# Loading the first batch, w1 and w2 ahead of w3 and w_out, and forming W3·w_out after the first chunk's stage one

## The chip, the cores and the metric

The kernel runs on one core of one Trainium2 chip. The metric is the device time of one execution in microseconds (us). Five engines work side by side, each through its own list of instructions in order: TensorE (PE, with its weight loads as PEld), VectorE (DVE), ScalarE (ACT), GpSimd (POOL) and SyncE (SP), which here issues nearly all DMAs.

## The reference

Attention with a softmax on q along the head dimension and a softmax on k along the sequence, and then a multiplicative feed-forward network on the result:

```python
q_s = softmax(q, axis=-1); k_s = softmax(k, axis=2)      # per batch and head
kv  = einsum('bhsd,bhse->bhde', k_s, v)
x   = einsum('bhsd,bhde->bhse', q_s, kv)                 # 8 batches, 8 heads, 576 x 64
x   = x.transpose(0, 2, 1, 3).reshape(4608, 512)
out = (((x @ w1) * (x @ w2)) @ w3) @ w_out               # d_ff = 1024, float32 out
```

## The kernel before

Everything is computed in f16 with f32 sums in PSUM. The product W3·w_out (1024 x 512, called W3O here, in eight tiles) is formed once, so that the network is two stages: stage one (`s1`) makes a·b for 512 tokens from x and 128 columns of w1 and of w2; stage two (`s2`) multiplies it by W3O for 128 tokens and stores them. The 4608 tokens are nine chunks of 512; they straddle the eight batches of 576.

**Attention of one batch.** Heads lie in two halves i = 0, 1 of four. `exp_q`, `exp_k` (ScalarE, L121 and L114), `sum_q` (VectorE, L133), `norm_q` (a reciprocal at L138 and a product on GpSimd at L140, tile eqn), `cast_v` (v to f16, L126). The normalised q is transposed into qsT, for batch 0 on TensorE (`piece_t`, L175, with a copy at L177) and for all others by a DMA transpose that SP issues (`dma_t`, L180). `piece_kv` (L154) makes kv, which VectorE normalises (L159, L163); `piece_x` (L192) makes x transposed, and ScalarE or VectorE copies it to the tile xT (L198, L200). `pieces(b)` are kv, x of half 0 and x of half 1.

**The weights.** w1 and w2 come in quarters of 256 columns (`load_w12`, L87), and are cast in four blocks each by three engines (`cast_w`, L94). w3 comes in eight row tiles (`load_w3`, L105), is cast (`w3_c`, L280), transposed on TensorE (`w3_t`, L292, copy at L297) and multiplied by the cast w_out (`wo_c`, L286) in `w3_mm` (L302).

**What sets the order.** The order is written by hand (`manual_schedule`): each engine does its instructions in the order of the program text. All loads pass through one ring of 12 staging slots ("st"); a load waits until the slot of the twelfth load before it has been read. Each DMA of SP also waits for the eighth DMA before it. In PSUM there are two "att" buffers of two banks each (transposes, kv, x), three "pab" buffers (stage one, W3O, alternate s2 tiles) and one "po". `warm(n)` are matmuls on zeros (L210) that nothing reads.

Before, SP issues w3 and w_out first (L311 to L318), then batch 0 (L355), w1 and w2 (L374), batch 1 (L398), the transposes of batch 1 (L444), batch 2 (L446). TensorE forms W3O while these arrive (L327 to L365), then does the attention of batch 0 (L379 to L401), stage one of chunk 0 with the exponentials of batch 1 between its last tiles (L421 to L443), and s2 of chunk 0 with kv and x of batch 1 between (L448 to L463).

From chunk 1 on, a loop (L506) runs eight s1 tiles and, one chunk behind, four s2 tiles; after each of these 12 places it calls `step()` (L471). A step takes the next of ten elementwise pieces of a batch (six for q, four for k and v), and puts the later work of the batch into `due`: its `dma_t` three steps after the product, loads, and `pieces` some steps after the tenth. Two steps are made ahead of the loop (L501).

Of the kernel before, what the change touches and what calls it, by code (L numbers as in the profile page):

```python
# [8 lines left out]
F32 = mybir.dt.float32  # L9
# [7 lines left out]
def kernel(  # L17
# [11 lines left out]
    nc = tc.nc  # L29
# [3 lines left out]
    P = 128  # L33
# [3 lines left out]
    N_FT = Fd // P  # L37
# [21 lines left out]
    def pAtt(shape, dtype):  # L59
        return psum.tile(shape, dtype, tag="att", name="att", bufs=2)  # L60

    def pAB():
        return psum.tile([P, CH], F32, tag="pab", name="pab", bufs=3)

    def pO():
        return psum.tile([P, C], F32, tag="po", name="po", bufs=1)
# [7 lines left out]
    def load_qkv(b, which, i, halves=False):  # L74
        src = {"q": q, "k": k, "v": v}[which]
        t = slot([P, 2, R * D])
        ap = src[b, 4 * i:4 * i + 4].rearrange("(h g) (s r) d -> (g s) h (r d)", g=2, r=R)
        for sl in (slice(0, 1), slice(1, 2)) if halves else (slice(0, 2),):
            nc.sync.dma_start(out=t[:, sl], in_=ap[:, sl])
        qkv32[(which, b, i)] = t  # L80
# [22 lines left out]
    def load_w3(ft):  # L103
        t = slot([P, Fd])
        nc.sync.dma_start(out=t, in_=moe_w3[ft * P:(ft + 1) * P, :])  # L105
        w32[("3", ft)] = t
# [11 lines left out]
    def exp_q(b, i, hh):  # L118
        if hh == 0:
            eqs[(b, i)] = attn.tile([P, R, 2, D], F16, tag="eq", name="eq", bufs=2)  # L120
        nc.scalar.activation(  # L121
            out=eqs[(b, i)][:, :, hh, :],
            in_=qkv32[("q", b, i)][:, hh].rearrange("p (r d) -> p r d", r=R), func=AF.Exp)
# [80 lines left out]
                lambda: (piece_x(b, 0, 0, 5), piece_x(b, 0, 5, 9)),  # L204
                lambda: (piece_x(b, 1, 0, 5), piece_x(b, 1, 5, 9, *[vcopy][b > 2:]))]

    def warm(n, att=False):
        wp = pAtt([P, 2, CH], F32)[:, 0] if att else pAB()
        for _ in range(n):
            nc.tensor.matmul(wp, lhsT=zero[:, 0:P], rhs=zero, start=True, stop=True)  # L210

# [63 lines left out]
    def w3_c(ft, *copies):  # L275
        w316s[ft] = attn.tile([P, Fd], F16, tag="w316", name="w316", bufs=3)
        n = Fd // len(copies)
        for m, copy in enumerate(copies):
            sl = slice(m * n, (m + 1) * n)
            copy(out=w316s[ft][:, sl], in_=w32[("3", ft)][:, sl])  # L280

    def wo_c(i, *copies):
        n = C // len(copies)
        for m, copy in enumerate(copies):
            sl = slice(m * n, (m + 1) * n)
            copy(out=wosb[i][:, :, sl], in_=w32[("o", i)][:, :, sl])  # L286

    def w3_t(ft):
        w316 = w316s[ft]
        tp = pAtt([P, N_FT, P], F16)  # L290
        for gt in range(N_FT):
            nc.tensor.transpose(tp[:, gt, :], w316[:, gt * P:(gt + 1) * P], ident)  # L292
        if ft < 4:
            w3T = attn.tile([P, R, P], F16, tag="qsT", name="qsT", bufs=4)
        else:
            w3T = attn.tile([P, R, P], F16, tag="eqn", name="eqn", bufs=4)
        nc.vector.tensor_copy(out=w3T[:, 0:N_FT, :], in_=tp)  # L297
        w3Ts[ft] = w3T

    def w3_mm(wps, ft, gts):  # L300
        for gt in gts:
            nc.tensor.matmul(wps, lhsT=w3Ts[ft][:, gt, :], rhs=wosb[gt // 2][:, gt % 2, :],  # L302
                             start=(gt == 0), stop=(gt == N_FT - 1))
# [4 lines left out]

    LOADS = [("q", 0), ("q", 1), ("k", 0), ("v", 0), ("k", 1), ("v", 1)]

    for ft in range(3):  # L311
        load_w3(ft)
    load_wo(0)
    load_w3(3)
    for i in range(1, 4):
        load_wo(i)
    for ft in range(4, 8):
        load_w3(ft)  # L318
    nc.vector.memset(zero, 0.0)
    make_identity(nc, ident)  # L320
    for t in v16buf:
        nc.gpsimd.memset(t[:, :, :, 64:65], 1.0 / SC)
    for t in kvbd:
        nc.gpsimd.memset(t, 0.0)


    warm(14)  # L327
    for ft in range(3):
        w3_c(ft, vcopy, acopy)
        w3_t(ft)  # L330
        warm(1)
    wo_c(0, pcopy, acopy)
    wps = [pAB(), pAB(), pAB(), pO()]
    for ft in range(3):
        w3_mm(wps[ft], ft, (0, 1))
    w3_c(3, vcopy, acopy)
    w3_t(3)
    wo_c(1, pcopy, acopy)
    for ft in range(3):
        w3_mm(wps[ft], ft, (2, 3))  # L340
    w3_mm(wps[3], 3, range(4))
    wo_c(2, pcopy, acopy)
    wo_c(3, pcopy, acopy)
    for ft in range(4):
        w3_mm(wps[ft], ft, (4, 5))
    w3_c(4, vcopy, acopy)
    w3_c(5, pcopy)
    for ft in range(4):
        w3_mm(wps[ft], ft, (6, 7))
        nc.scalar.copy(out=W3O[ft], in_=wps[ft])  # L350
        if ft == 1:
            w3_t(4)
    w3_t(5)
    w3_c(6, pcopy)
    for which, i in LOADS:  # L355
        load_qkv(0, which, i, halves=(which, i) == ("v", 1))
    for ft in range(4, N_FT):
        if ft == 4:
            w3_c(7, pcopy)
        wp = pO() if ft % 2 else pAB()  # L360
        w3_mm(wp, ft, range(4))
        if ft + 2 < N_FT:
            w3_t(ft + 2)
        w3_mm(wp, ft, range(4, N_FT))
        nc.scalar.copy(out=W3O[ft], in_=wp)  # L365
        if ft in (5, 6):
            for hh in range(2):
                exp_q(0, ft - 5, hh)
                sum_q(0, ft - 5, hh)
            norm_q(0, ft - 5, nc.gpsimd)  # L370
        if ft == 6:
            exp_k(0, 0, 0)
            exp_k(0, 0, 1)
    for qt in range(4):  # L374
        load_w12(0, qt)
        load_w12(1, qt)


    piece_t(0, 0)  # L379
    cast_v(0, 0, vcopy, slice(0, 1))  # L380
    cast_v(0, 0, acopy, slice(1, 2))
    warm(1)
    piece_kv(0, 0)
    warm(1)
    piece_t(0, 1)
    exp_k(0, 1, 0)
    exp_k(0, 1, 1)
# [2 lines left out]
    cast_v(0, 1, pcopy, slice(1, 2), slice(5, 9))  # L390
    warm(2)
    piece_x(0, 0, 0, 8)
    warm(2)
    piece_kv(0, 1)
    warm(1)
    cast_w(0, 0, (pcopy, pcopy, acopy, vcopy), cols=slice(0, P))
    cast_w(0, 0, (pcopy, pcopy, acopy, acopy), cols=slice(P, 2 * P))
    for which, i in LOADS:  # L398
        load_qkv(1, which, i)

# [1 line left out]
    cast_w(1, 0, (pcopy, pcopy, acopy, vcopy))  # L402
    cast_w(0, 1, (vcopy, vcopy, pcopy))

    def elementwise_steps(b, cv=pcopy):
        st = []
        for i in range(2):
            st += [lambda i=i: exp_q(b, i, 0),
                   lambda i=i: (sum_q(b, i, 0), exp_q(b, i, 1)),
                   lambda i=i: (sum_q(b, i, 1), norm_q(b, i, nc.gpsimd))]  # L410
        for i in range(2):
            st += [lambda i=i: exp_k(b, i, 0),
                   lambda i=i: (cast_v(b, i, cv), exp_k(b, i, 1))]
        return st

    def more_casts():
        cast_w(0, 1, (acopy,), ((1, 0),))
        cast_w(1, 1, (pcopy, pcopy, acopy, acopy))

    ew = elementwise_steps(1, vcopy)  # L420
    s1_pair(0, more_casts)  # L421
    piece_x(0, 0, 8, 9)
    piece_x(0, 1, 8, 9)
# [9 lines left out]
    cast_w(1, 3, (vcopy, pcopy, pcopy))  # L433
    s1(0, 5)
    cast_w(1, 3, (acopy,), ((1, 0),))
    s1(0, 6)
    ew[0]()
    ew[1]()
    s1(0, 7)
    ew[2]()  # L440
    ew[3]()
    ew[4]()
    ew[5]()  # L443
    dma_t(1, 0)  # L444
    dma_t(1, 1)
    for which, i in LOADS:  # L446
        load_qkv(2, which, i)
    s2(0, 0, alt=True)  # L448
    ew[6]()
    ew[7]()  # L450
    s2(0, 1)
    piece_kv(1, 0)
    exp_k(1, 1, 0)
    exp_k(1, 1, 1)
    cast_v(1, 1, vcopy, slice(0, 1))
    cast_v(1, 1, acopy, slice(1, 2))
    s2(0, 2, alt=True)
    piece_kv(1, 1)
    piece_x(1, 0, 0, 5)
    piece_x(1, 0, 5, 9, vcopy)  # L460
    s2(0, 3)
    piece_x(1, 1, 0, 5)
    piece_x(1, 1, 5, 9, vcopy)  # L463


    todo = [(b, n, f) for b in range(2, B) for n, f in enumerate(elementwise_steps(b))]
# [4 lines left out]
    def step():  # L471
        t = slot_no[0]
        slot_no[0] += 1
        for f in due.pop(t, []):
            f()
        if not todo:
            return
        b, n, f = todo.pop(0)
        f()
        if b == 2 and n == 9:  # L480
            for m in range(2):
                due.setdefault(t + 1 + m, []).append(lambda m=m: load_qkv(4, *LOADS[m]))
        if 2 < b < B - 2:
            for m in LOADS_AFTER.get(n, ()):
                due.setdefault(t + 1, []).append(lambda m=m: load_qkv(b + 2, *LOADS[m]))
        if n in (2, 5):
            if b == 2:
                if n == 5:
                    due.setdefault(t + 3, []).append(lambda: (dma_t(2, 0), dma_t(2, 1)))
                    for m in range(6):  # L490
                        due[t + 3].append(lambda m=m: load_qkv(3, *LOADS[m]))
            else:
                due.setdefault(t + 3, []).append(lambda: dma_t(b, n // 3))
            if b == 3 and n == 5:
                for m in range(2, 6):
                    due.setdefault(t + 3 + m // 4, []).append(lambda m=m: load_qkv(4, *LOADS[m]))
        if n == 9:
            for d, p in zip((2, 3, 4) if b == 2 else (2, 4, 6), pieces(b)):
                due.setdefault(t + d, []).insert(0, p)

    step()  # L501
    step()

# [42 lines left out]
```

The softmax here doesn't subtract the row's maximum and nothing guards it: scores larger than these inputs give would overflow.

## Time and profile before

| | |
|---|---|
| time, median of 3 runs | 256.56 us (255.31 to 257.47) |
| the profiled execution | 257.47 us, span 255.7 us |
| mean granted TensorE clock | 0.976 |
| busy: PE, PEld, DVE, ACT, POOL | 237.6, 113.0, 130.1, 114.2, 64.4 us |
| read and written | 38.80 and 9.44 MB, 189 GB/s over the span |
| last matmul ends, span ends | 251.6, 255.7 us |

The span runs from the first to the last instruction; the time has some 1.8 us more around it. A line of the timeline gives start, duration, engine, line of the kernel, operation, output<-input by names (numbers left out), type and shape and count; in brackets the engine's idle time ahead of it and what ended it. "PEclk" is the share of the full TensorE clock that was granted. SPq is SP's queue: such a line is the issue of a DMA. A matmul of 512 columns is shown as 380 ns long, but the next one starts 216 ns later, since they overlap. w_0_75 to w_3_78 are the quarters of w1 in f16, w_0_79 to w_3_82 those of w2.

### The profile page before, as it was taken

How to read it: one execution, taken by the hardware profiler on the slowest of the kernel's cores; microseconds unless marked ns; L12 is line 12 of the kernel's file. 1: busy time of each engine (PE TensorE's matmuls, PEld its weight loads, DVE VectorE, ACT ScalarE, POOL GpSimd, SP SyncE). 2: the span in 40 equal slices, each digit the busy share in tenths (PEclk: the TensorE clock that was granted, in tenths of full speed). 3: DMA queues.
4: the chain of work that ended last, by engine and by line, in shares of the span. 5: the costliest groups of instructions: out<-in, count | busy, mean ns of one | idle time of the engine just before them, and what ended most of it. 6: DMA issues, size and time to landing. Idle time of an engine off the chain costs nothing.

```text
span 255.7 us, 3879 instructions
## 1 busy us (share of the span) xinstructions
PE 237.6 (93%) x1394; PEld 113.0 (44%) x1394; DVE 130.1 (51%) x238; ACT 114.2 (45%) x197; POOL 64.4 (25%) x64
## 2 busy tenths in 40 slices
PE   8699489978995999999999999999999999999993
PEld 3355244434442344544544544544544444444442
DVE  1614648596561663754854754753533443443342
ACT  3354848771763546375374375375151222112200
POOL 3142784042090314242134144044000000000000
PEclk9999979999999599999999999999999999999998
DMA  6999999609999999999999975135311122112334
GB/s 250 388 408 390 362 348 383 225 3 149 393 318 299 398 280 273 380 401 253 335 237 248 360 98 107 36 70 111 65 44 41 41 61 64 42 41 51 73 82 124
DMA packets 42052, 52.62 MB, mean 206 GB/s; under 512 B 18865, under 2 KB 23217, under 8 KB 42033
## 3 DMA queue, kind: packets, MB, share of 16 engines
q1 hardware_dynamic: 41632, 51.85, 68.1%
q10 hardware_dynamic: 400, 0.52, 0.6%
q8 instruction: 11, 0.18, 0.3%
q14 instruction: 9, 0.07, 0.1%
HBM read 38.80 MB, written 9.44 MB: 189 GB/s over the span
## 4 chain that ended last, share of the span: by engine, by line
PE 65%; DMA 2%; ACT 1%; DVE 1%; issue 0%; SPq 0%; ACTq 0%
PE pab L218 39%; PE po L261 20%; PE att L192 3%; PE att L154 2%; PE pab L261 2%; DMA st<-in_q_dram 2%; ACT xT L200 1%; DVE abT L228 0%; SPq L180 0%; DVE kvbd_87 L163 0%; ACT a_970 L223 0%; DVE osb L263 0%; DVE rc L159 0%; ACT eq L121 0%; ACTq L223 0%
## 5 line engine op out<-in xcount | busy, mean ns | idle before, releaser
L140 POOL TENSOR_TENSOR eqn<-eq,dr 128x1152 f16<-128x1152 f16 x16 | 34.3, 2150 | 95.7 <-DVE dr L138 66.1
L261 PEld LDWEIGHTS <-abT 128*128 128x128 f16 x296 | 28.6, 98 | 32.3
L263 DVE TENSOR_SCALAR osb<-po 128x512 f32<-128x512 f32 (+1 forms) x32 | 21.8, 682 | 24.3 <-PE po L261 23.2
L200 ACT CAST xT<-att 128x640 f16<-128x640 f32 (+3 forms) x28 | 16.6, 635 | 21.6 <-PE att L192 21.5
L133 DVE TENSOR_REDUCE ds<-eq 128x9 f32<-128x576 f16 x32 | 23.5, 744 | 3.0 <-ACT eq L121 2.8
L121 ACT ACTIVATE eq<-st 128x576 f16<-128x576 f32 x32 | 21.2, 688 | 6.1 <-DMA st<-in_q_dram 6.1
L218 PE MATMUL pab<-xT,w_3_82 128*128 128x512 f16 x72 | 18.6, 380 | 2.9 <-ACT a_970 L223 2.9
L114 ACT ACTIVATE ek<-st 128x576 f16<-128x576 f32 x32 | 20.7, 682 | 0.0
L218 PE MATMUL pab<-xT,w_0_75 128*128 128x512 f16 x72 | 20.0, 407 | 0.2
L218 PE MATMUL pab<-xT,w_0_79 128*128 128x512 f16 x72 | 18.3, 381 | 0.5 <-ACT a_847 L223 0.5
L218 PE MATMUL pab<-xT,w_1_80 128*128 128x512 f16 x72 | 18.5, 379 | 0.0
L218 PE MATMUL pab<-xT,w_1_76 128*128 128x512 f16 x72 | 18.5, 379 | 0.0
L218 PE MATMUL pab<-xT,w_2_77 128*128 128x512 f16 x72 | 18.5, 379 | 0.0
L218 PE MATMUL pab<-xT,w_3_78 128*128 128x512 f16 x72 | 18.5, 379 | 0.0
L218 PE MATMUL pab<-xT,w_2_81 128*128 128x512 f16 x72 | 18.5, 379 | 0.0
L218 PEld LDWEIGHTS <-w_3_82 128*128 128x128 f16 x72 | 7.0, 98 | 11.5 <-issue 3.1
L261 PE MATMUL po<-W3O_91,abT 128*128 128x512 f16 (+1 forms) x32 | 12.1, 377 | 0.0
L261 PE MATMUL po<-W3O_92,abT 128*128 128x512 f16 (+1 forms) x32 | 12.0, 376 | 0.0
L261 PE MATMUL po<-W3O_93,abT 128*128 128x512 f16 (+1 forms) x32 | 12.0, 376 | 0.0
L261 PE MATMUL po<-W3O_94,abT 128*128 128x512 f16 (+1 forms) x32 | 12.0, 376 | 0.0
L261 PE MATMUL po<-W3O_95,abT 128*128 128x512 f16 (+1 forms) x32 | 12.0, 376 | 0.0
L261 PE MATMUL po<-W3O_96,abT 128*128 128x512 f16 (+1 forms) x32 | 12.0, 376 | 0.0
(297 smaller groups left out, 354.8 us busy)
## 6 DMA issues: line engine op xcount, KB each, us to landing
st<-in_q_dram SPq DMA_DIRECT2D x16, 576.0 KB, 8.6
st<-in_k_dram SPq DMA_DIRECT2D x16, 576.0 KB, 7.5
st<-in_v_dram SPq DMA_DIRECT2D x15, 576.0 KB, 8.9
out_dram<-osb SPq DMA_DIRECT2D x67, 128.0 KB, 2.4
st<-in_moe_w_dram SPq DMA_DIRECT2D x16, 512.0 KB, 9.6
st<-in_moe_w_out_dram SPq DMA_DIRECT2D x4, 512.0 KB, 9.3
st<-in_v_dram SPq DMA_DIRECT2D x2, 288.0 KB, 10.8
out_dram<-osb ACTq DMA_DIRECT2D x3, 128.0 KB, 2.6
```

The lines of the kernel that those rows point to most:

```text
L114: nc.scalar.activation(out=eks[(b, i)][:, :, hh, :], in_=qkv32[("k", b, i)][:, hh].rearrange("p (r d) -> p r d", r=R), func=AF.Exp)
L121: nc.scalar.activation(out=eqs[(b, i)][:, :, hh, :], in_=qkv32[("q", b, i)][:, hh].rearrange("p (r d) -> p r d", r=R), func=AF.Exp)
L133: nc.vector.tensor_reduce(out=dss[(b, i)][:, :, hh], in_=eqs[(b, i)][:, :, hh, :], axis=AX.X, op=ALU.add)
L140: eng.tensor_tensor(out=eqn.rearrange("p r h d -> p (r h) d"), in0=eqs[(b, i)].rearrange("p r h d -> p (r h) d"), in1=dr[:, :, None].broad ...
L154: nc.tensor.matmul(kvp[:, g, 0:130].rearrange("p (h e) -> p h e", h=2), lhsT=eks[(b, i)][rows, r].rearrange("p h d -> p (h d)"), rhs=v16bu ...
L192: nc.tensor.matmul(xps[g][:, 0:n].rearrange("p (r s) -> p r s", s=SP), lhsT=kv2[:, g, :], rhs=qsT[:, r0:r1, 64 * g:64 * g + 64], start=Tru ...
L200: (copies[0] if copies else nc.scalar.copy)(out=dst, in_=xp[:, :, 0:n])
L218: nc.tensor.matmul(p, lhsT=wsb[qt][:, ct, fo:fo + P], rhs=xT[:, ct, t0:t0 + CH], start=(ct == 0), stop=(ct == N_CT - 1))
L261: nc.tensor.matmul(po[:, 0:n1 - n0], lhsT=abT[(j, ft)][:, tb * P:(tb + 1) * P], rhs=W3O[ft][:, n0:n1], start=(ft == 0), stop=(ft == N_FT - 1))
L263: nc.vector.tensor_scalar(out=osb[:, n0:n1], in0=po[:, 0:n1 - n0], scalar1=ISC, scalar2=None, op0=ALU.mult)
```

## The change

The first loads are now batch 0, then six quarters of w1 and w2, then the last two quarters, w3 tiles 0 to 2, w_out pair 0, w3 tile 3 and the other pairs of w_out; w3 tiles 4 to 7 and batch 1 follow after batch 0's attention in the text. TensorE makes 26 warm-up matmuls, the attention of batch 0 and stage one of chunk 0, and puts the transposes of w3 tiles 0 to 2 around the last two stage-one tiles. Then it forms W3O, four tiles at once over the four pairs of w_out (with the transposes of w3 tile 3 behind the first pair), then tiles 4 to 7 one by one. GpSimd casts all w3 tiles but tile 5 and half of tile 3, and two of the four w_out pairs alone; before, w3 tiles 0 to 4 and all pairs were shared. The exponentials, sums and products of batch 1 lie among W3O tiles 4 to 7. The first two loads of batch 2 are issued ahead of batch 1's transposes, the other four behind them. Four more steps are made ahead of the loop, among s2 tiles 2 and 3 of chunk 0, and q of batch 3 is loaded between them. In `step()`, the transposes of batch 2 are due one by one, and its pieces 2, 6 and 7 steps after its tenth step, not 2, 3 and 4. The two column pieces of the last stored tile (L258) are as they were, and so is the order of `piece_kv(0, 0)` and `piece_t(0, 1)`.

The core of the diff, with what is only moved cut out:

```diff
+    for which, i in LOADS:
+        load_qkv(0, which, i, halves=(which, i) == ("v", 1))
+    load_w12(0, 0)
...
+    load_w12(1, 2)
...
+    warm(26)
+    for i in range(2):
+        for hh in range(2):
+            exp_q(0, i, hh)
+            sum_q(0, i, hh)
+        norm_q(0, i, nc.gpsimd)
+    exp_k(0, 0, 0)
+    exp_k(0, 0, 1)
+    load_w12(0, 3)
+    load_w12(1, 3)
     for ft in range(3):
         load_w3(ft)
...
-    warm(14)
-    for ft in range(3):
-        w3_c(ft, vcopy, acopy)
-        w3_t(ft)
-        warm(1)
-    wo_c(0, pcopy, acopy)
...
-    warm(1)
+    warm(6)
     piece_kv(0, 0)
-    warm(1)
     piece_t(0, 1)
...
+    for ft in range(3):
+        w3_c(ft, pcopy)
     s1(0, 6)
-    ew[0]()
-    ew[1]()
+    w3_t(0)
+    w3_t(1)
     s1(0, 7)
...
+    w3_t(2)
+    wo_c(0, pcopy, acopy)
+    w3_c(3, pcopy, acopy)
+    wo_c(1, pcopy, acopy)
+    wo_c(2, pcopy)
+    wo_c(3, pcopy)
+    wps = [pAB(), pAB(), pAB(), pO()]
+    for gp in range(4):
+        for ft in range(4):
+            if gp == 0 and ft == 3:
+                w3_t(3)
+                continue
+            if gp == 1 and ft == 3:
+                w3_mm(wps[ft], ft, (0, 1))
+            w3_mm(wps[ft], ft, (2 * gp, 2 * gp + 1))
+            if gp == 3:
+                nc.scalar.copy(out=W3O[ft], in_=wps[ft])
+                if ft == 1:
+                    w3_t(4)
+        if gp == 0:
+            w3_c(4, pcopy)
+            w3_c(5, vcopy)
...
+    for ft in range(4, N_FT):
...
+        for n in {4: (0, 1), 5: (4,)}.get(ft, ()):
+            ew[n]()
+        w3_mm(wp, ft, range(4, N_FT))
+        nc.scalar.copy(out=W3O[ft], in_=wp)
+        for n in {4: (2, 3), 5: (5, 6), 6: (7,), 7: ()}[ft]:
+            ew[n]()
+        if ft == 6:
+            exp_k(1, 1, 0)
+    exp_k(1, 1, 1)
+    load_qkv(2, *LOADS[0])
+    load_qkv(2, *LOADS[1])
     dma_t(1, 0)
     dma_t(1, 1)
-    for which, i in LOADS:
+    for which, i in LOADS[2:]:
         load_qkv(2, which, i)
...
-            if b == 2:
-                if n == 5:
-                    due.setdefault(t + 3, []).append(lambda: (dma_t(2, 0), dma_t(2, 1)))
-                    for m in range(6):
-                        due[t + 3].append(lambda m=m: load_qkv(3, *LOADS[m]))
-            else:
-                due.setdefault(t + 3, []).append(lambda: dma_t(b, n // 3))
+            due.setdefault(t + 3, []).append(lambda: dma_t(b, n // 3))
+            if b == 2 and n == 5:
+                for m in range(2, 6):
+                    due[t + 3].append(lambda m=m: load_qkv(3, *LOADS[m]))
...
-            for d, p in zip((2, 3, 4) if b == 2 else (2, 4, 6), pieces(b)):
+            for d, p in zip((2, 6, 7) if b == 2 else (2, 4, 6), pieces(b)):
...
+    step()
+    step()
+    s2(0, 2, alt=True)
+    pc[1]()
+    load_qkv(3, *LOADS[0])
+    load_qkv(3, *LOADS[1])
+    step()
+    step()
+    s2(0, 3)
+    pc[2]()
     step()
     step()
```

More of the change, by code (lines that the diff above doesn't have):

```diff
@@ L205, in pieces, with warm @@
                 lambda: (piece_x(b, 1, 0, 5), piece_x(b, 1, 5, 9, *[vcopy][b > 2:]))]
-    def warm(n, att=False):
-        wp = pAtt([P, 2, CH], F32)[:, 0] if att else pAB()
+    def warm(n):
+        wp = pAB()
         for _ in range(n):
@@ L309 @@
     LOADS = [("q", 0), ("q", 1), ("k", 0), ("v", 0), ("k", 1), ("v", 1)]
+    for which, i in LOADS:
+        load_qkv(0, which, i, halves=(which, i) == ("v", 1))
+    load_w12(0, 0)
+    load_w12(1, 0)
+    load_w12(0, 1)
+    load_w12(1, 1)
+    load_w12(0, 2)
+    load_w12(1, 2)
+    nc.vector.memset(zero, 0.0)
+    make_identity(nc, ident)
+    for t in v16buf:
+        nc.gpsimd.memset(t[:, :, :, 64:65], 1.0 / SC)
+    for t in kvbd:
+        nc.gpsimd.memset(t, 0.0)
+    warm(26)
[8 more added lines that the diff above has]
+    load_w12(1, 3)
     for ft in range(3):
@@ L316 @@
         load_wo(i)
[L317 to L324, printed above, removed]
-    warm(14)
-    for ft in range(3):
-        w3_c(ft, vcopy, acopy)
-        w3_t(ft)
-        warm(1)
-    wo_c(0, pcopy, acopy)
[L333 to L354, printed above, removed]
-    for which, i in LOADS:
[L356 to L376, printed above, removed]
     piece_t(0, 0)
@@ L392 @@
     piece_x(0, 0, 0, 8)
-    warm(2)
     piece_kv(0, 1)
-    warm(1)
     cast_w(0, 0, (pcopy, pcopy, acopy, vcopy), cols=slice(0, P))
     cast_w(0, 0, (pcopy, pcopy, acopy, acopy), cols=slice(P, 2 * P))
+    warm(1)
+    for ft in range(4, 8):
+        load_w3(ft)
     for which, i in LOADS:
@@ L403 @@
     cast_w(0, 1, (vcopy, vcopy, pcopy))
[L405 to L414, printed above, removed]
     def more_casts():
@@ L418, in more_casts @@
         cast_w(1, 1, (pcopy, pcopy, acopy, acopy))
-    ew = elementwise_steps(1, vcopy)
     s1_pair(0, more_casts)
@@ L435 @@
     cast_w(1, 3, (acopy,), ((1, 0),))
+    for ft in range(3):
+        w3_c(ft, pcopy)
     s1(0, 6)
-    ew[0]()
-    ew[1]()
+    w3_t(0)
+    w3_t(1)
     s1(0, 7)
[L440 to L443, printed above, removed]
+    w3_t(2)
[20 more added lines that the diff above has]
+            w3_c(5, vcopy)
@@ new lines, with elementwise_steps @@
+    w3_t(5)
+    w3_c(6, pcopy)
+    def elementwise_steps(b, cv=pcopy):
+        st = []
+        for i in range(2):
+            st += [lambda i=i: exp_q(b, i, 0),
+                   lambda i=i: (sum_q(b, i, 0), exp_q(b, i, 1)),
+                   lambda i=i: (sum_q(b, i, 1), norm_q(b, i, nc.gpsimd))]
+        for i in range(2):
+            st += [lambda i=i: exp_k(b, i, 0),
+                   lambda i=i: (cast_v(b, i, cv), exp_k(b, i, 1))]
+        return st
+    ew = elementwise_steps(1, vcopy)
@@ new lines @@
+    pc = pieces(1)
+    for ft in range(4, N_FT):
+        if ft == 4:
+            w3_c(7, pcopy)
+        wp = pO() if ft % 2 else pAB()
+        w3_mm(wp, ft, range(4))
+        if ft + 2 < N_FT:
+            w3_t(ft + 2)
+        for n in {4: (0, 1), 5: (4,)}.get(ft, ()):
[6 more added lines that the diff above has]
+            exp_k(1, 1, 0)
@@ L444 @@
+    exp_k(1, 1, 1)
+    load_qkv(2, *LOADS[0])
+    load_qkv(2, *LOADS[1])
     dma_t(1, 0)
     dma_t(1, 1)
-    for which, i in LOADS:
+    for which, i in LOADS[2:]:
         load_qkv(2, which, i)
     s2(0, 0, alt=True)
[L449 to L454, printed above, removed]
     cast_v(1, 1, vcopy, slice(0, 1))
     cast_v(1, 1, acopy, slice(1, 2))
[L457 to L460, printed above, removed]
@@ L461 @@
-    s2(0, 3)
-    piece_x(1, 1, 0, 5)
-    piece_x(1, 1, 5, 9, vcopy)
+    s2(0, 1)
+    pc[0]()
     todo = [(b, n, f) for b in range(2, B) for n, f in enumerate(elementwise_steps(b))]
```

## The prediction

> **What bounds the kernel now.** I read the slices of the page first, because they say where TensorE is not dense and what the DMA does there.
>
> ```profile
> PE   8699489978995999999999999999999999999993
> PEclk9999979999999599999999999999999999999998
> DMA  6999999609999999999999975135311122112334
> GB/s 250 388 408 390 362 348 383 225 3 149 393 318 299 398 280 273 380 401 253 335 237 248 360 98 107 36 70 111 65 44 41 41 61 64 42 41 51 73 82 124
> ```
>
> A slice is 6.4 us; I count from 0. From slice 14 on PE is full, and the DMA has slack later: the last 160 us are bound by TensorE. All that can move lies in the first 14 slices, and there the DMA is full except in slices 7 to 9 (45 to 64 us), where it sinks to 3 GB/s. The clock is down in slice 5 and in slice 13. The timeline gives the landmarks:
>
> ```profile
> 10.14 1.46 PE L302 MATMUL pab<-wo_83,qsT 128*128 128x512 f16 x6
> ...
> 38.07 1.89 PE L218 MATMUL pab<-xT,w_0_75 128*128 128x512 f16 x8
> ...
> 41.27 1.27 POOL L94 CAST w_3_82<-st 64x512 f16<-64x512 f32 x2 [0.86 <-DMA st<-in_moe_w_dram]
> ...
> 56.49 3.89 SPq L180 DMA_TRANSPOSE qsT<-eqn  x2
> ...
> 60.49 1.98 SPq L79 DMA_DIRECT2D st<-in_q_dram  x2
> ...
> 64.26 1.99 PE L218 MATMUL pab<-xT,w_0_75 128*128 128x512 f16 x8
> ```
>
> W3O is formed from 10 us, stage one of chunk 0 starts at 38.07, of chunk 1 at 64.26. The last w2 quarter lands at 41.27, so the start is paced by 14.0 MB (w3, wo, batch 0, w1, w2) at 350 to 400 GB/s. At 56.49 SP, which works in order, comes to the two transposes of batch 1, and only behind them, at 60.49, to the loads of batch 2. That is the hole in the DMA. What it costs stands in the chain of waits, in order of time:
>
> ```profile
> 76.12 0.66 SPq L180
> ...
> 76.87 4.11 DMA st<-in_q_dram
> ...
> 81.06 0.04 ACT eq L121
> ...
> 81.66 0.58 ACT a_970 L223
> ...
> 86.39 5.25 PE pab L218 x16
> 91.64 1.73 PE po L261 x8
> ```
>
> The load of q of batch 3 is issued at 76.87 and lands at 80.98; its exponential (L121) stands ahead of the PSUM copy a_970 in ScalarE's queue, so TensorE waits 2.85 us for a_970. Then 16 matmuls take 5.25 us in place of 3.45. The windows (PE busy, PEld, DVE, ACT, POOL, then granted clock, DMA share, GB/s) show why:
>
> ```profile
> 80.00:81.00 1.00, 0.00 (x0) 0.00 (x0) 0.00 (x0) 0.00 (x0) 0.00 (x0) 1.00 1.00 357
> ...
> 87.00:88.00 1.00, 1.00 (x4) 0.36 (x3) 0.56 (x2) 0.21 (x1) 0.85 (x1) 0.50 1.05 387
> ```
>
> The clock is halved from 83.5 to 89.5 us. From 91.48 (first s2 tile of chunk 1) the chain is PE without a gap to 251.63, and a tail of 4.1 us follows.
>
> **What the Trainium skill says.** "TensorE: Matmul & The Clock Gate", Part 1: the PE clock is halved after a free-running activity window of about 3.4 us with too little work, and comes back after a busy one. The trace agrees: 0.50 after the idle of 79.4 to 82.3 us and again at 32 to 35.9 us. The same page, in its note on queue depths, calls ScalarE and VectorE strict FIFOs; the 2.85 us behind L121 are that. "DMA: Bandwidth & Descriptors", Queues, rings and completion order: each DMA engine consumes one issuer's descriptors in ring order. So a transpose queued behind loads runs after them; the load issued at 76.87 behind two transposes, which took 4.1 us for 576 KB, agrees.
>
> **The change, part by part.** PE's useful work is the same: no matmul is added but warm-ups (35 for 24), all in the first 16 us, where PE waits for data anyway; without that cover they would cost 11 x 0.216 = 2.4 us. The storing of the last tile (L258) and the order of kv(0,0) and the second query transposes are already in the kernel before and are no part of the sum. What moves is the order.
>
> *Start.* Loads land, by the trace, at 4.1 us for the first and, from the third on, every 1.33 us (512 KB of w3 or wo), 1.47 (576 KB) or 1.49 (512 KB of w1, w2). With q, k, v first: q at 4.3 and 5.8, k0 8.6, v0 10.1, k1 11.6, v1 13.1, then w1 and w2 quarters at 14.6, 16.1, ... 25.1. Exponentials (0.63 each in a pair), sums (0.74), a product on GpSimd (2.1 each) give the first normalised queries at 8.9 and 11.0; kv(0,0) follows v0's cast at 11.1 to 11.8, kv(0,1) v1's at 13.7 to 14.4, its normalisation ends at 15.3, x(0,1) and copies at 16.6. Stage one starts at **16.0** on the first two column blocks, against 38.07. It then follows the weights: quarter n arrives at 16.1, 19.1, 22.1, 25.1, its last cast 1.3 us later, and stage one asks for them at 17.8, 20.6, 24.0, 27.5. The 32 casts are the same; they keep up.
>
> *W3O moved behind.* 64 matmuls at 0.216 are 13.8 us and 8 groups of transposes at 0.45 are 3.6: together 17.4. Before, they lay under the wait for data; now they stand in the row. By 38 us PE has done 22 us of stage one and W3O where it had done 17.4 of W3O: the start alone is worth about 4 us, since W3O's cover is lost.
>
> *Row to chunk 1.* 16.0 + 13.8 (64 stage-one matmuls) + 17.4 + 6.9 (32 of stage two) + 1.15 (kv of batch 1) + 0.98 (its x) + 0.1 = 56.3. Waits inside: w3 and wo land from 26.4 to 40.9, each 1 us before PE asks for it after its cast; batch 1's loads land up to 49, as before (the same 17.6 MB). ScalarE's queue puts exponentials of batch 1 ahead of the W3O copies, so the seventh copy ends near 46.3 and the last near 49.8: 0.4 us of PE wait. The transposes for batch 1 are issued at 47 and 49, but lie behind batch 2's q loads (to 52) and land near 55.5 and 57.8; PE asks at 54.8 and 57.3: 1 to 1.5 us. I take 2.2, so chunk 1 starts at **58.5**, against 64.26: 5.8 gained. Moved past in SP's queue: q of batch 2 goes ahead of the transposes, q of batch 3 ahead of the stores of the fourth tile; GpSimd now casts all w3 (1.04 each) and much of wo, at 26 to 42 us, where it had nothing else.
>
> *Chunk 1 to s2(1,0).* Dense it is 13.8 + 1.15 + 0.98 + 3.45 = 19.4; before it took 91.48 - 64.26 = 27.2, of which 2.85 is the wait, about 3.3 the halved clock, the rest small gaps. After, the DMA has no hole: batch 2's k and v follow the transposes and land at 59 to 63.5, batch 3's q at 65 and 66.5; ScalarE reaches their exponentials at 62 and 65. No wait as long as that of before, and so no halved clock. The trace of before can't show whether these land in time; from below the cost is 0, from above the 6.2 us of before. I take 1.5.
>
> *After that* the elementwise steps run four slots earlier relative to PE; this is hidden under a full PE.
>
> Sum: 5.8 + (27.2 - 19.4) - 1.5 = **12.1 us** off 257.47, the profiled run (255.7 of span and 1.8 around it): 245.4. That run is 0.9 above the median of 256.56; from the median it is 244.5. I say **245.0**.
>
> **Rivals.** (a) *Half of it is given back.* One batch comes late once: a wait of 2.85 and a halved clock of 3.3 in chunk 1, as now. 12.1 + 1.5 - 6.2 = 7.4, so 249 to 250, and up to 254 with a second halved window (1.7 to 3.3) at the start, where PE has gaps. For it: slacks of 1 to 3 us on a DMA that is full. Against: the loads no longer wait behind the transposes' release. (b) *Nothing to measure.* The load stream breaks because SP, in order, waits for a staging slot (12 of them; w3's fifth needs all casts of w1's third quarter). A pause of 5 us moves chunk 1 to 63.5, and with (a)'s loss the gain is about 2: 255. Against: I find each slot free some 5 us or more before its turn. (c) *Slower.* The DMA backlog persists, and ScalarE's in-order queue meets a late load once in each of batches 2, 3 and 4: three times 6.2 is 18.6, less 12.1 + 1.5, so about 5 slower, 262. It decides from the point at which loads lie more than 4 us behind my list when chunk 1 starts, since one tile of stage one (1.73) and my slack of 2 are then used up; it needs the loads to run at some 350 instead of 390 GB/s over the first 17.6 MB. Against: the same loads ran at 385 to 396 outside w1 and w2.
>
> **How the numbers follow.** My forecast 0.62, (a) 0.20, (b) 0.08, (c) 0.10. The forecast's own range is 241 (no wait at all: 56.3 + 19.4 puts s2(1,0) at 75.7, 15.8 us earlier) to 249. With (a) it reaches to 254, which leaves out 0.18. A measurement of this kernel tells about 1% from no change; faster by over 1% is below 254: 0.62 + 0.20 = 0.82; within 1% 0.08; slower 0.10.
>
> **What would show it.** In the profile after: stage one (L218) begins near 16 us; no DMA slice below 200 GB/s before 60 us; the first stage-one matmul of chunk 1 near 58.5; no stretch with clock 0.50 after 20 us; s2(1,0) near 79. Wrong would be: a first stage-one matmul after 20 us; PE waiting on L223 behind L121 or L114 for over 2 us; x(1,0) waiting for its transpose beyond 58.

## The result and the profile after

The changed kernel takes 243.49 us (median of 4 runs, 243.23 to 243.92), the kernel before 256.58 (4 runs, 255.31 to 257.47): a ratio of 0.9495, 95% interval 0.9452 to 0.9538. The profiled execution took 243.72 us with a span of 241.9; against the profiled one of before that is 13.75 us less, of which the span holds 13.8. Single executions of a kernel that take over 1.5% longer than its shortest are left out of the ratios here and below, and kept in the medians and ranges.

The profiled execution of before, at 257.47 us, is longer than the medians of the kernel before in the runs below (256.3 to 256.9). It has two stretches of halved clock, 31.9 to 35.3 and 83.1 to 89.9 us; what follows compares with it, and experiments 8 and 9 say what these stretches are worth.

The slices of the page after, each now 6.05 us:

```profile
PE   8989999999999999999999999999999999999993
PEclk9999999999999999999999999999999999999999
DMA  6999999999999999999999514411223222123234
GB/s 237 388 348 355 403 398 396 391 282 329 336 231 384 301 362 392 389 260 395 298 308 331 120 43 95 93 43 43 46 58 71 44 46 45 43 59 71 45 88 130
```

The 4 and the 5 in the first half of the PE row are gone, the clock has no dip in the row, and the DMA has no hole: its lowest slice before the loads end is 231 GB/s (67 to 73 us, where transposes run), where slice 8 had 3. The landmarks in the timeline of TensorE:

```profile
15.97 1.89 PE L218 MATMUL pab<-xT,w_0_75 128*128 128x512 f16 x8
...
31.81 1.73 PE L302 MATMUL pab<-wo_83,qsT 128*128 128x512 f16 x6
...
54.78 0.65 PE L192 MATMUL att<-qsT,kvbd_89 128*128 128x320 f16 x4
...
57.48 2.09 PE L218 MATMUL pab<-xT,w_0_75 128*128 128x512 f16 x8
...
68.77 1.02 PE L218 MATMUL pab<-xT,w_2_81 128*128 128x512 f16 x4 [0.17 <-ACT a_994 L223]
...
77.79 0.38 PE L261 MATMUL po<-W3O_91,abT 128*128 128x512 f16 x1
```

Stage one of chunk 0 starts at 15.97 (before 38.07), of chunk 1 at 57.48 (64.26), the first s2 tile of chunk 1 at 77.79 (91.48). So 6.78 us are gained up to chunk 1, 6.91 in chunk 1, and 0.1 in all the rest. The line at 68.77 is the place of the old 2.85 us wait on ScalarE: 0.17 is left. x of batch 1 (54.78) has no wait in brackets: the transposes were there.

What TensorE waits for after 16 us, in the view of waits (us in total, times, longest):

```profile
PE pab L218 <- ACT a_994 L223: 0.2, 1, 0.2
PE att L292 <- POOL w_457 L280: 0.2, 1, 0.2
```

Only these two are listed, 0.3 us in all (0.17 and 0.16 in the timeline). The queue of ScalarE tells the other half, that the loads of batch 1 come in as W3O is being finished (start, duration, in brackets the idle time ahead and what ended it):

```profile
42.66 1.26 ACT L121 ACTIVATE eq<-st 128x576 f16<-128x576 f32 x2 [1.75 <-DMA st<-in_q_dram]
...
48.65 0.68 ACT L114 ACTIVATE ek<-st 128x576 f16<-128x576 f32 x1 [0.70 <-DMA st<-in_k_dram]
49.24 0.57 ACT L443 CAST W3O_98<-po 128x512 f16<-128x512 f32 x1
```

ScalarE waits for q and for the second k of batch 1, and the W3O copies stand behind these; TensorE is just busy enough not to notice.

### The profile page after: what moved, and what is told of

The parts are those of the page before. It is cut to its first block, busy times and chain, and to the rows that moved or that the text cites. A ratio compares the mean times of both kernels' runs of the same rounds, so it can differ in the third digit from the quotient of the medians.

```text
span 241.9 us, 3885 instructions
## 1 busy us (share of the span) xinstructions
PE 234.7 (97%) x1405; PEld 112.9 (47%) x1405; DVE 128.5 (53%) x233; ACT 111.2 (46%) x192; POOL 69.6 (29%) x68
## 4 chain that ended last, share of the span: by engine, by line
PE 85%; DMA 5%; DVE 4%; POOL 1%; ACT 1%; issue 1%; DVEq 0%; ACTq 0%; POOLq 0%
PE pab L218 46%; PE po L261 23%; DMA st<-in_moe_w_dram 4%; PE att L154 3%; PE pab L302 3%; PE pab L261 3%; PE att L192 3%; PE po L302 2%; DMA st<-in_q_dram 1%; PE att L292 1%; POOL eqn L140 1%; DVE abT L228 1%; DVE qsT L177 1%; DVE ds L133 1%; ACT eq L121 1%
## 5 line engine op out<-in xcount | busy, mean ns | idle before, releaser
L218 PE MATMUL pab<-xT,w_2_81 128*128 128x512 f16 x72 | 18.5, 379 | 0.2 <-ACT a_994 L223 0.2
L218 PE MATMUL pab<-xT,w_1_76 128*128 128x512 f16 x72 | 18.5, 379 | 0.0
L218 PE MATMUL pab<-xT,w_3_78 128*128 128x512 f16 x72 | 18.5, 379 | 0.0
L218 PE MATMUL pab<-xT,w_2_77 128*128 128x512 f16 x72 | 18.5, 379 | 0.0
L218 PE MATMUL pab<-xT,w_3_82 128*128 128x512 f16 x72 | 18.5, 379 | 0.0
L218 PE MATMUL pab<-xT,w_1_80 128*128 128x512 f16 x72 | 18.5, 379 | 0.0
L218 PE MATMUL pab<-xT,w_0_75 128*128 128x512 f16 x72 | 18.3, 379 | 0.1
L218 PE MATMUL pab<-xT,w_0_79 128*128 128x512 f16 x72 | 18.0, 379 | 0.0
L261 PE MATMUL po<-W3O_91,abT 128*128 128x512 f16 (+1 forms) x32 | 12.1, 377 | 0.0
L261 PE MATMUL po<-W3O_94,abT 128*128 128x512 f16 (+1 forms) x32 | 12.0, 376 | 0.0
L261 PE MATMUL po<-W3O_95,abT 128*128 128x512 f16 (+1 forms) x32 | 12.0, 376 | 0.0
L261 PE MATMUL po<-W3O_96,abT 128*128 128x512 f16 (+1 forms) x32 | 12.0, 376 | 0.0
L261 PE MATMUL po<-W3O_97,abT 128*128 128x512 f16 (+1 forms) x32 | 12.0, 376 | 0.0
L261 PE MATMUL po<-W3O_98,abT 128*128 128x512 f16 (+1 forms) x32 | 12.0, 376 | 0.0
L261 PE MATMUL po<-W3O_92,abT 128*128 128x512 f16 (+1 forms) x32 | 12.0, 376 | 0.0
```

What stands on the lines that cost most here:

```text
L218: nc.tensor.matmul(p, lhsT=wsb[qt][:, ct, fo:fo + P], rhs=xT[:, ct, t0:t0 + CH], start=(ct == 0), stop=(ct == N_CT - 1))
L261: nc.tensor.matmul(po[:, 0:n1 - n0], lhsT=abT[(j, ft)][:, tb * P:(tb + 1) * P], rhs=W3O[ft][:, n0:n1], start=(ft == 0), stop=(ft == N_FT - 1))
```

## The experiments

Each kernel was run several times beside runs of the kernel before on the same chip; the ratios are to those. The kernel before had medians of 256.27, 256.52 and 256.87 us in the three sets. The changed kernel is not in these sets: where a kernel is set against it, that is its median of 243.49 us and its profile. The other parts of the change (the four more steps, the later pieces of batch 2, its transposes one by one, the casts on GpSimd) were not tested apart.

**1. The order of the loads alone, in the kernel before.** W3O stays first.

```diff
+    for which, i in LOADS:
+        load_qkv(2, which, i)
     dma_t(1, 0)
     dma_t(1, 1)
-    for which, i in LOADS:
-        load_qkv(2, which, i)
     s2(0, 0, alt=True)
...
     piece_x(1, 1, 5, 9, vcopy)
+    load_qkv(3, *LOADS[0])
+    load_qkv(3, *LOADS[1])
...
-                    for m in range(6):
+                    for m in range(2, 6):
                         due[t + 3].append(lambda m=m: load_qkv(3, *LOADS[m]))
```

> The kernel before with only SP's order changed: all six loads of batch 2 ahead of batch 1's transposes, and q of batch 3 ahead of batch 2's transposes; W3O still first. Theory (the loss in chunk 1 comes from loads that stand behind transposes in SP's in-order queue): the wait of 2.85 us and the halved clock in chunk 1 go, chunk 1 to s2(1,0) takes about 20.5 us in place of 27.2, less up to 1 us since batch 1's transposes now land behind six loads: 250 to 251. Rival (the loss belongs to the order of the start, W3O first, and can't be mended without it): 255 to 257.

Measured: 250.88 us, ratio 0.9807 (0.9732 to 0.9882). The timeline of TensorE in this kernel:

```profile
60.31 1.14 PE L192 MATMUL att<-qsT,kvbd 128*128 128x320 f16 x4 [2.59 <-DMA qsT<-eqn]
...
64.35 12.46 PE L218 MATMUL pab<-xT,w 128*128 128x512 f16 x56
...
85.09 1.89 PE L261 MATMUL po<-W3O,abT 128*128 128x512 f16 x8
```

Chunk 1 to its first s2 tile takes 20.74 us (before 27.22, after 20.31): nearly the whole second half of the gain, without any change of the start. The parts that were not tested apart are all missing here, so in chunk 1 little is left for them. x of batch 1 now waits 2.59 us for a transpose that stands behind six loads; up to 1 had been expected.

**2. One of these moves alone.** In the kernel before only q of batch 3 is moved ahead of batch 2's transposes (the second and third part of the diff above); the hole in the DMA stays.

> The kernel before with one move only: q of batch 3 ahead of batch 2's transposes; batch 2's loads stay behind batch 1's transposes, so the hole in the DMA stays. Theory (the wait of chunk 1 is the place of this one load, the hole by itself is hidden): 250 to 252, as with both moves. Rival (the hole is what costs; without filling it the load of q of batch 3 is late anyway): 255 to 257.

Measured: 253.77 us, ratio 0.9898 (0.9867 to 0.9929), between the two. Its profiled execution, at 251.1 us the shortest of 20, has the full clock throughout. Chunk 1 takes 23.65 us in it:

```profile
61.51 12.44 PE L218 MATMUL pab<-xT,w 128*128 128x512 f16 x56
...
77.22 1.02 PE L218 MATMUL pab<-xT,w 128*128 128x512 f16 x4 [1.15 <-ACT a L223]
78.73 0.43 PE L192 MATMUL att<-qsT,kvbd 128*128 128x320 f16 x2 [0.48 <-DVE kvbd L163]
79.48 0.89 PE L192 MATMUL att<-qsT,kvbd 128*128 128x256 f16 x4 [0.32 <-DVE kvbd L163]
...
85.16 1.89 PE L261 MATMUL po<-W3O,abT 128*128 128x512 f16 x8
```

Of the 6.5 us that both moves save in this stretch, in these profiles, the q loads bring 3.6: 2.3 by shorter waits up to the last stage-one tile (from the start of chunk 1 to the end of its wait 15.7 us in place of 18.0), and 1.3 behind it, where the clock is no longer halved. The other 2.9 are the hole. With batch 2 late, SP comes to the loads of q of batch 3 only at 71.20 (in experiment 1 at 65.98), their exponential still keeps ScalarE waiting for 3.44 us, up to 76.01, and TensorE waits 1.15 us behind it; so the rival was right in part. Then kv and x of batch 2 crowd at the end of chunk 1, and TensorE waits 1.75 us more for the short steps of VectorE and ScalarE between them. Neither theory had it alone. By the ratios the q loads bring 1.0% and both moves 1.9%; the two intervals overlap a little, so the split rests on one profile of each.

**3. The same loads put back, in the changed kernel.**

```diff
-    load_qkv(3, *LOADS[0])
-    load_qkv(3, *LOADS[1])
...
-                for m in range(2, 6):
+                for m in range(6):
                     due[t + 3].append(lambda m=m: load_qkv(3, *LOADS[m]))
```

> The changed kernel with q of batch 3 loaded behind the transposes of batch 2, as in the kernel before. Theory: these loads are then issued near 70 us and land near 74, ScalarE reaches their exponential at 66, so TensorE waits some 5 us or more and its clock is halved: 250 to 254, half or more of the gain is gone. Rival (the gain comes from the start alone, the place of this load is of no account): 243 to 245.

Measured: 249.75 us, ratio 0.9765 (0.9704 to 0.9826); 6.3 us of the gain are gone, and the time is just under the expected 250 to 254. The wait is back at its old place:

```profile
73.42 4.44 PE L218 MATMUL pab<-xT,w 128*128 128x512 f16 x12 [4.86 <-ACT a L223]
```

4.86 us of wait, and 12 matmuls in 4.44 us where 12 take 2.75 in the changed kernel, since the clock is halved behind it. 4.86 + 1.69 is 6.55, near the 6.3 of the time.

**4. The transposes of batch 1 behind all of batch 2, in the changed kernel.**

```diff
-    load_qkv(2, *LOADS[0])
-    load_qkv(2, *LOADS[1])
+    for which, i in LOADS:
+        load_qkv(2, which, i)
     dma_t(1, 0)
     dma_t(1, 1)
-    for which, i in LOADS[2:]:
-        load_qkv(2, which, i)
```

> The changed kernel with all six loads of batch 2 ahead of batch 1's transposes, in place of two. Theory (one issuer's transfers run in the order of issue): the transposes come four loads of 1.5 us later, x of batch 1 waits for them 4 to 5 us, chunk 1 starts near 62 in place of 57.5: 247 to 250. Rival (a transpose finds room beside loads, its place is of no account): 243 to 245.

Measured: 252.07 us, ratio 0.9853 (0.9787 to 0.9919): 8.6 us lost, more than expected; chunk 1 starts at 66.47, where 62 had been expected.

```profile
61.18 1.12 PE L192 MATMUL att<-qsT,kvbd 128*128 128x320 f16 x4 [5.25 <-DMA qsT<-eqn]
62.10 3.62 PE L261 MATMUL po<-W3O,abT 128*128 128x512 f16 x8
...
66.47 7.21 PE L218 MATMUL pab<-xT,w 128*128 128x512 f16 x32
```

The wait of 5.25 us is the queue in order, as expected: SP issues the first transpose at 49.67, 2.3 us later than in the changed kernel, and it lands 11.4 us after that. The half clock behind the wait was not in the expectation: eight matmuls take 3.6 us there in place of 1.9. The Trainium skill ("DMA: Bandwidth & Descriptors", Queues, rings and completion order) says that each DMA engine consumes descriptors in ring order; this run agrees, in that four loads of 576 KB put ahead of the transposes made TensorE wait 5.25 us for them.

**5. Less TensorE work in W3O.** 16 of the 64 matmuls are made; the sums over six of eight row blocks are left out.

```diff
         for gt in gts:
-            nc.tensor.matmul(wps, lhsT=w3Ts[ft][:, gt, :], rhs=wosb[gt // 2][:, gt % 2, :],
-                             start=(gt == 0), stop=(gt == N_FT - 1))
+            if gt % 4 == 0:
+                nc.tensor.matmul(wps, lhsT=w3Ts[ft][:, gt, :], rhs=wosb[gt // 2][:, gt % 2, :],
+                                 start=(gt == 0), stop=(gt == 4))
```

> The changed kernel with 16 of the 64 matmuls that form W3O (the sums over six of the eight row blocks are left out); all loads, casts and transposes stay. 48 matmuls of 0.216 are 10.4 us of TensorE. As the prediction put it (W3O has lost its cover and stands in the row): about 10 us faster, 233. Rival (W3O lies under the loads of w3, w_out and batch 1, whose last k lands at 48.6 us and ends the last W3O copy at 49.8 whatever TensorE does): 242 to 245, no gain, perhaps a little loss by a halved clock.

Measured: 244.11 us, ratio 0.9551 (0.9491 to 0.9611): nothing gained by 10.4 us less of TensorE work. The timeline shows the wait that takes its place:

```profile
46.28 0.59 PE L303 MATMUL po<-wo,eqn 128*128 128x512 f16 x2 [2.37 <-ACT W3O L444]
...
50.04 0.38 PE L261 MATMUL pab<-W3O,abT 128*128 128x512 f16 x1 [1.66 <-ACT W3O L444]
```

The last matmul of the first s2 tile runs at 50.04, in the changed kernel at 49.86. It waits for the last W3O copy, that copy for the exponential of the second k, and this for its load.

**6. Less load.** w3 tiles 4 to 7 are not loaded; a constant tile is cast and transposed in their place, so half of W3O isn't computed from w3.

```diff
-    for ft in range(4, 8):
-        load_w3(ft)
...
+    nc.vector.memset(w3fix, 0.5)
...
-            copy(out=w316s[ft][:, sl], in_=w32[("3", ft)][:, sl])
+            copy(out=w316s[ft][:, sl], in_=(w3fix if ft > 3 else w32[("3", ft)])[:, sl])
```

> The changed kernel without the loads of w3 tiles 4 to 7 (a constant tile is cast and transposed in their place, so half of W3O is not computed from w3): 2.1 MB, 5.3 us of DMA, less ahead of batch 1; TensorE does all it did. Theory (up to 50 us TensorE and the loads end together, TensorE is dense from 16 us): no gain, 242.5 to 244. Rival (the loads alone set the pace): about 5 us faster, 238 to 239.

Measured: 243.62 us, ratio 0.9526 (0.9468 to 0.9583): nothing gained by 2.1 MB less either. From the start of stage one to chunk 1 it takes 41.58 us in the profile, in the changed kernel 41.51.

**7. Both.** The diffs of 5 and 6 together, leaving out what each leaves out.

> Both at once: no loads of w3 tiles 4 to 7 (a constant tile in their place) and only 16 of the 64 matmuls that form W3O. Theory (two covers of equal length): only now the time falls, by about the 5.3 us of DMA: 238 to 239.5. Rival (something else, such as the queue of ScalarE or the casts on GpSimd, sets the pace up to 50 us): 242 to 244.

Measured: 240.09 us, ratio 0.9394 (0.9342 to 0.9445): 3.4 us faster than the changed kernel, between the two expected ranges. So the two covers lie over each other, as the theory has it; 5.3 had been expected. In the profile TensorE now waits for GpSimd's casts (1.6 + 1.1 us) and VectorE's copies (1.4 + 0.8), and from 38.5 to 41.9 us its clock is halved. Which of these takes the missing 2 us was not tested.

**8. The idle stretch of chunk 1 filled, in the kernel before.**

```diff
         a16 = s1_a(pa)
+        if (j, fb) == (1, 7):
+            wp = pO()
+            for _ in range(13):
+                nc.tensor.matmul(wp, lhsT=zero[:, 0:P], rhs=zero, start=True, stop=True)
```

> The kernel before with 13 matmuls on zeros (2.8 us) between the two halves of the last stage-one tile of chunk 1, where TensorE waits for ScalarE. Theory (the clock is halved because of this idle stretch, and the half clock costs 3.3 us more): the wait stays, the clock stays at 1.00, about 3 us faster: 253 to 254. Rival (the clock falls for another reason, or the added work is paid in full): 256 to 259.

Measured: 256.02 us, ratio 1.0024 (0.9986 to 1.0062): no gain, as the rival's range has it, but not for its reasons. The clock did stay at 1.00 in the profile:

```profile
84.00:86.00 2.00, 1.22 (x7) 0.28 (x5) 1.84 (x8) 1.10 (x3) 0.00 (x0) 1.00 1.03 402
```

But PE is busy for 1.22 of these 2 us: at full clock it waits for kv's normalisation and the copies of x (VectorE 1.84 of 2). From the start of chunk 1 to its first s2 tile it took 25.9 us in place of 27.2. The wait ends 18.0 us after the start of chunk 1 in both, so the added matmuls were not paid for; from there to the s2 tile it takes 7.9 us in place of 9.2. So the clock does follow the idle stretch, and the halved clock in that place costs some 1.3 us in this pair of profiles, not 3.3. That the execution as a whole shows no gain is not explained.

**9. The start of the kernel before filled.** Eight matmuls on zeros ahead of the first query transposes, six in place of one ahead of kv.

```diff
+    warm(8)
     piece_t(0, 0)
...
-    warm(1)
+    warm(6)
     piece_kv(0, 0)
```

> The kernel before with 13 more matmuls on zeros in the two gaps ahead of batch 0's attention (8 ahead of the first query transposes, 6 in place of 1 ahead of kv), 2.8 us of TensorE where it waits. Theory (the halved clock of 32 to 36 us comes from these gaps and costs about 2.4 us, since batch 0's attention is a chain of short steps): 253 to 254.5, and less spread from run to run. Rival (the halved clock there is hidden by the other engines, as in chunk 1): 255.5 to 257.

Measured: 255.01 us, ratio 0.9961 (0.9928 to 0.9994), between the two; its executions range from 253.8 to 257.7 us, those of the kernel before beside them from 253.9 to 259.6. Its profile, from the first transposes on:

```profile
28.66 0.68 PE L175 MATMUL att<-ident,eqn 128*128 128x128 f16 x9
...
35.78 3.62 PE L218 MATMUL pab<-xT,w 128*128 128x512 f16 x16
...
80.42 1.87 PE L218 MATMUL pab<-xT,w 128*128 128x512 f16 x4 [3.52 <-ACT a L223]
```

The same stretch in the kernel before:

```profile
29.10 0.68 PE L175 MATMUL att<-ident,eqn 128*128 128x128 f16 x9 [1.85 <-POOL eqn L140]
...
31.38 0.75 PE L154 MATMUL att<-v_0_73,ek 64*128 64x130 f16 x18 [1.39 <-DVE v_0_73 L126]
```

And in experiment 1, whose instructions up to here are those of the kernel before:

```profile
28.29 0.68 PE L175 MATMUL att<-ident,eqn 128*128 128x128 f16 x9 [1.85 <-POOL eqn L140]
...
35.42 3.62 PE L218 MATMUL pab<-xT,w 128*128 128x512 f16 x16
```

From the first transposes to stage one it takes 7.12 us with the fill and 8.97 in the kernel before, so the halved clock costs 1.9 us there. But experiments 1 and 2, without the fill and with the same gaps ahead, take 7.13 and 7.12 with the full clock, and experiment 8, again with the same gaps, 9.95 with the clock halved. The gaps are thus followed by a halved clock in some executions and not in others; the one profile of the filled kernel can't show that the fill prevents it. That the filled kernel is faster by less than 1.9 us fits.

In chunk 1 of this profile the wait on ScalarE has grown from 2.85 to 3.52 us and the clock halves behind it as before; chunk 1 as a whole takes 26.67 us, no longer than the 27.22 of before.

**10. The warm-up matmuls of the changed kernel left out.**

```diff
-    warm(26)
+    warm(2)
...
-    warm(6)
+    warm(1)
     piece_kv(0, 0)
```

> The changed kernel with 3 matmuls on zeros ahead of batch 0's kv in place of 32 (26 + 6). As the prediction put it (they lie where TensorE waits for data and cost nothing; what they bring was not said): 243 to 244. Theory now (they keep the clock up; without them it is still halved when the attention of batch 0 and the first tiles of stage one run, up to some 20 us): 245 to 247.

Measured: 244.81 us, ratio 0.9585 (0.9534 to 0.9636), 1.3 us slower than the changed kernel's median, just under the 245 to 247 that was expected. The two intervals overlap, so the profile has to say it:

```profile
9.12 1.14 PE L175 MATMUL att<-ident,eqn 128*128 128x128 f16 x9 [6.90 <-POOL eqn L140]
11.87 1.16 PE L154 MATMUL att<-v,ek 64*128 64x130 f16 x18 [1.18 <-DVE v L126]
...
17.43 3.61 PE L218 MATMUL pab<-xT,w 128*128 128x512 f16 x16
```

The first transposes and kv take 1.14 and 1.16 us in place of 0.68 and 0.69, and stage one starts 1.46 us later; at the start of chunk 1 0.9 us of that are left (58.39 against 57.48).

## Why the prediction was right

The time lies in the range and 1.5 us below the forecast. By the steps of the prediction:

- *Start at 16.0*: 15.97. The list of landings held to a few tenths.
- *Row to chunk 1, 56.3 + 2.2*: 57.48. The row was right but for 1.2 us, where 2.2 had been set down for waits. Only 0.3 of the 1.2 are waits in the trace; the rest is spread over small stretches, of which the six W3O matmuls at 31.81, 1.73 us long where six later ones take 1.46, are one. The transposes of batch 1 were in time, where 1 to 1.5 us had been set down for them. Experiment 4 shows that this term was a near thing.
- *Chunk 1, 19.4 + 1.5*: 20.31, so 0.9 in place of 1.5. That the place of the loads of q of batch 3 makes most of the wait is shown from both sides (experiments 2 and 3), that the hole has its own share by experiment 2 against 1. The prediction read the hole's cost as that one load; it was both.
- *Sum*: 12.1 against 13.75 in the profiled executions. The two allowances, 2.2 and 1.5, were 1.0 and 0.6 too large.
- *"The start alone is worth about 4 us, since W3O's cover is lost"*: this reason fell, though the number it served did not. W3O is still covered, now by the loads of w3, w_out and batch 1: taking three quarters of its matmuls away gives nothing (experiment 5), taking a part of the loads away gives nothing (6), and both give 3.4 us (7). The sum came out right because both covers end together at 50 us: adding up PE's row gives the time whichever of them is taken for the limit. In so far the number was better than its reason.
- *"About 3.3 the halved clock" in chunk 1*: mis-sized. The one filled kernel shows some 1.3 there (8), most of it being hidden by VectorE and ScalarE. What the prediction did not set apart is the halved clock at the start, 31.9 to 35.3 us in the record of the clock (it read 32 to 35.9). It costs 1.9 us in the profiled execution of before (9), is part of what the first half gained there, and comes in some executions only. In experiment 2's execution, which has the same start at full clock, chunk 1 begins at 61.51, only 4.0 us later than in the changed kernel.
- *The load behind two transposes, 4.1 us for 576 KB*: this does not show the order of the queue. The very first load of the kernel before (512 KB), with nothing ahead of it, takes 3.4 us from its issue at 0.74 to its use at 4.12. Experiment 4 is what shows the order.
- *Warm-ups cost nothing*: right in the changed kernel's profile, where the first transposes follow them without a wait, but with little to spare. In the profile of experiment 6 they take 8.70 us in place of 7.79, and stage one starts 0.66 us later. They also bring something: 1.3 us by the medians, 0.9 up to chunk 1 in the profiles (10).
- *Rivals*: (a), one late batch, and (b), a broken load stream, did not come about: no wait over 0.2 us after 16 us, no DMA slice of the loads under 231 GB/s. (c), a backlog, neither. That (a) was near is shown by experiments 3 and 4: the two q loads put behind two transposes, or the transposes behind four more loads, cost 6 to 9 us.

The first half of the gain, in the two profiles, is thus: stage one starts 22.1 us earlier, W3O takes 17.4 of that back, and 2.1 us of small gaps that stood between 38 and 64 us (1.43 for v's cast, 0.51 and 0.37 for kv and a transpose are the largest) are gone. The largest of them in the timeline of before:

```profile
57.23 0.69 PE L154 MATMUL att<-v_1_74,ek 64*128 64x130 f16 x18 [1.43 <-DVE v_1_74 L126]
```

In the timeline after, nearly all of batch 1's exponentials and casts run under W3O. That this is why the gaps are gone was not tested.

## What to carry to other kernels

Where one issuer's queue is in order, put loads that a later stage needs ahead of transfers that wait for computed data, but no more of them than the next consumer of those transfers can bear: count the bytes on both sides. Order the loads by when TensorE first needs each, and put work that needs late weights where the next batch's loads and its elementwise steps need a cover. Before calling work exposed, take it away, and take its cover away, and then both.

## What the runs showed of the hardware that was not expected

The executions of the kernel before that the ratios count ran between 253.5 and 257.6 us in these sets, with a mean granted clock of 0.990 at the short end and 0.980 at the long one; the changed kernel, in four executions, between 243.2 and 243.9 with 0.997 to 1.000. A kernel with gaps of 1 to 3 us on TensorE pays a varying amount for them: the same gaps of 1.85 and 1.4 us at the start were followed by a halved clock in two profiled executions (before, experiment 8) and not in two others (1, 2), which is 1.9 to 2.8 us between them. The Trainium skill ("TensorE: Matmul & The Clock Gate", Part 1) calls the clock's window free-running, which fits; that this makes the whole spread is a reading of the clocks, not an experiment.

In the kernel without warm-ups the first transposes ran at half speed (1.14 us for nine, in place of 0.68), while the record of the granted clock shows 1.00 there. At the start of this execution the durations tell the clock, the record doesn't.
